# Attention in tiles of 128 queries and one head of each pair, with 64x64 score products

## The chip, the core and the metric

The kernel runs on one core of a Trainium2 chip. The metric is the device time of one execution in microseconds (us), the median of several. The core has a matrix engine (TensorE, PE in the profile; its weight loads stand apart as PEld), three engines for elementwise work (VectorE or DVE, ScalarE or ACT, GpSimd or POOL), and SyncE (SP), which here issues nearly all DMAs. Each engine runs its own list of instructions in order and waits on semaphores for the others. TensorE reads SBUF and writes PSUM; a PSUM tile holds up to 128 partitions by 512 float32.

## The reference, cut to what matters

A windowed attention (2 batches, 8 heads, 768 positions, 64 dimensions a head) is followed by a mixture of experts and a feed-forward layer. Only the attention is touched:

```python
def _attn_ref(q, k, v):
    B, H, S, D = q.shape                      # 2, 8, 768, 64
    block, window = (32, 16)
    nb = S // block                           # 24 blocks of 32 positions
    scale = 1.0 / np.sqrt(D)
    k_sum = k.reshape(B, H, nb, block, D).max(axis=3)
    v_sum = v.reshape(B, H, nb, block, D).mean(axis=3)
    scores_l = scale * np.matmul(q, k.transpose(0, 1, 3, 2))
    mask_l = np.abs(pos[:, None] - pos[None, :]) < window
    scores_s = scale * np.einsum('bhsd,bhnd->bhsn', q, k_sum) + np.log(block)
    scores_l_m = np.where(mask_l, scores_l, -1000000000.0)
    a = softmax(np.concatenate([scores_l_m, scores_s], axis=-1))   # 1e-9 added to the sum
    return np.matmul(a, np.concatenate([v, v_sum], axis=2))
```

The rows of the result go through a router (`logits = x @ w_gate`), experts and a feed-forward layer, whose code is the same before and after.

## The kernel before, in words

Attention works on blocks of 64 queries: such a block needs the 96 keys around it and the 24 block maxima, 120 columns in all. There are 24 blocks j (12 for each batch). `KW` holds for each pair of heads c (two heads of 64 dimensions make 128 partitions) and each block the 120 key columns; `VW` holds the 120 value rows in the same order.

`scores j h` (L272) computes 64 queries of two heads at once: the weights `QB` are a block diagonal of 128x128, with head 0's queries in one corner, head 1's in the other and zeros elsewhere, so that the 128 output rows are 64 queries of head 0 and 64 of head 1. `masked` (L283) adds the mask and takes the row maximum in one VectorE instruction for each pair; `exps` (L294) takes the exponential on ScalarE, one instruction for each pair, which sums the rows too. `norm` (L303) takes the reciprocal of the sums. `p_turn` (L308) transposes the weights on TensorE, `p_out` copies them out of PSUM, and `pv` (L319) multiplies them by the values of both heads (128 columns, of which each row uses 64). `pv_out` (L327) takes the two useful quarters of that product, multiplies them by the reciprocals and writes the output rows `xs`. `x_store` sends a tile of 128 rows to DRAM for the experts, `x_turn`, `x_out`, `logits` (L350) and `logits_out` make the router's logits of it.

Loads: `load` brings 128 partitions of two positions each (runs of 512 bytes), `load_tiles` 128 partitions of one position and 8 heads (runs of 256 bytes). `pairs` and `tiles` transpose them, `k_out` and `q_out` copy them into place, `k_max`, `k_ends` and `k_blocks` make the block maxima and fill the columns that neighbouring blocks share. `v_blocks`, `v_sum`, `v_rows`, `v_rows_out` and `v_means` make the value means and copy them to `VW`, the last of them by 24 DMAs.

The order of all this is written out by hand in the table `ORDER`, one word after the other; within an engine, instructions run in just that order. PSUM has two buffers for each of `ps` (scores), `pt` (turned weights), `po` (products with v) and `ptr` (all other). The router begins (L477) when the logits and the stores to DRAM are complete; the rest of the program follows from there.

Of the kernel before, what the change touches and what calls it, by code (L numbers as in the profile page):

```python
# [52 lines left out]
k_ends 0 1 1 pool; pairs q 0 1 0; pairs q 0 2 1; k_blocks 0 0 0 dve; k_max 0 1 1; load q 0 1 1; v_sum 0 0 0
pool; k_blocks 0 0 1 dve; v_sum 0 1 0 pool; scores 0 0; scores 0 1; q_out 0 1 0 act; load_tiles 1 0; scores 1 0;
scores 1 1; k_blocks 0 1 1 dve; load_tiles 1 1; q_out 0 2 1 act; masked 0 0; exps 0 0; pairs q 0 1 1; masked 0
1; scores 2 0; masked 1 0; exps 0 1; scores 2 1; masked 1 1; scores 3 0; scores 3 1; v_sum 0 0 1 dve; exps 1 0;
load_tiles 1 2; p_turn 0; k_blocks 0 1 0 dve; v_sum 0 1 1 pool; load_v 0 0; tiles 1 0 0; exps 1 1; p_turn 1;
load q 1 0 0; masked 3 0; masked 3 1; masked 2 0; q_out 0 1 1 act; p_out 0 dve; masked 2 1; exps 2 0; load q 1 1
0; scores 4 0; scores 4 1; exps 3 0; pairs q 0 2 0; k_ends 0 2 0 pool; k_out 1 0 0 act; k_ends 0 2 1 dve; exps 2
1; scores 5 0; masked 4 0; exps 3 1; q_out 0 2 0 dve; scores 5 1; p_turn 2; v_rows 0; masked 4 1; scores 6 0;  # L60
k_blocks 0 2 1 pool; tiles 1 0 1; exps 4 0; v_rows_out 0 act; exps 4 1; masked 5 0; exps 5 0; load q 1 0 1; norm
3; k_blocks 0 2 0 pool; masked 5 1; scores 6 1; p_out 1 dve; scores 7 0; p_out 2 act; scores 7 1; p_turn 4;
tiles 1 2 0; masked 6 0; masked 6 1; scores 8 0; scores 8 1; masked 7 0; k_out 1 0 1 act; tiles 1 1 1; exps 5 1;
k_out 1 2 0 act; v_means 0 0; p_out 4 dve; exps 6 0; masked 7 1; k_max 1 0 0; v_blocks 1; scores 9 0; p_turn 3;
k_out 1 1 1 act; exps 6 1; scores 9 1; exps 7 0; tiles 1 1 0; k_max 1 2 0; k_out 1 1 0 act; masked 8 0; masked 8
1; scores 10 0; tiles 1 2 1; p_out 3 act; k_max 1 0 1; k_max 1 1 1; p_turn 5; masked 9 0; masked 9 1; v_sum 1 0
1 pool; k_max 1 1 0; exps 7 1; norm 0; v_means 0 1; pv 0; scores 10 1; k_out 1 2 1 act; load q 1 2 0; norm 2;
exps 9 0; pairs q 1 0 1; pv 1; pv_out 0; k_max 1 2 1; load q 1 1 1; norm 1; k_ends 1 2 2 dve; k_ends 1 0 2 dve;
norm 7; q_out 1 0 1 act; p_turn 6; scores 11 0; norm 4; scores 11 1; p_out 5 act; exps 9 1; pairs q 1 1 0; pairs
q 1 0 0; load_v 0 1; q_out 1 0 0 act; q_out 1 1 0 act; pv_out 1; p_turn 7; v_sum 1 0 0 dve; masked 10 0; pv 2;  # L70
x_turn 0; x_out 0 dve; k_blocks 1 0 2 dve; exps 8 0; masked 10 1; exps 8 1; load q 1 2 1; pv_out 2; exps 10 0;
masked 11 0; norm 5; x_store 0; pv 3; pairs q 1 1 1; pv_out 3; logits 0; scores 12 0; v_means 0 2; q_out 1 1 1
act; norm 6; k_ends 1 1 2 dve; exps 10 1; logits_out 0 act; scores 12 1; p_out 6 act; pv 4; pv 5; pairs q 1 2 0;
masked 11 1; v_sum 1 1 0 pool; masked 12 0; masked 12 1; v_sum 1 1 1 pool; k_blocks 1 2 2 dve; exps 12 0; p_out
7 act; scores 13 0; scores 13 1; pv_out 4; exps 11 0; scores 14 0; masked 13 0; x_store 1; v_rows 1; load_v 1 1;
pv_out 5; p_turn 8; q_out 1 2 0 act; x_store 2; pv 6; v_rows_out 1 dve; exps 12 1; load_v 0 2; masked 13 1;
p_turn 9; pv_out 6; exps 11 1; scores 14 1; norm 10; masked 14 0; p_out 8 act; x_turn 2; pairs q 1 2 1; p_out 9
act; scores 15 0; p_turn 10; x_out 2 act; p_turn 11; masked 14 1; x_turn 1; norm 12; k_blocks 1 1 2 dve; exps 13
0; pv 7; p_out 11 dve; scores 15 1; exps 13 1; pv 8; norm 8; scores 16 0; masked 15 0; scores 16 1; masked 15 1;
x_out 1 act; pv_out 7; q_out 1 2 1 act; exps 14 0; masked 16 0; p_turn 13; p_out 13 dve; scores 17 0; scores 17  # L80
1; masked 16 1; pv_out 8; exps 15 0; logits 1; exps 16 0; norm 9; exps 14 1; p_out 10 act; x_turn 3; masked 17
0; scores 18 0; x_out 3 act; pv 9; load_v 1 0; logits_out 1 dve; masked 17 1; scores 19 0; logits 3; exps 15 1;
p_turn 12; masked 18 0; scores 18 1; exps 16 1; exps 18 0; scores 19 1; exps 17 0; logits 2; norm 11; p_out 12
dve; pv_out 9; p_turn 14; p_turn 15; pv 10; norm 16; masked 18 1; exps 17 1; masked 19 0; p_out 15 act; masked
19 1; logits_out 2 act; v_means 1 0; scores 20 0; norm 15; masked 20 0; exps 18 1; scores 21 0; exps 20 0; later
0; logits_out 3 act; p_out 14 act; x_store 3; pv_out 10; pv 11; scores 20 1; p_turn 16; exps 19 0; masked 21 0;
masked 20 1; norm 13; scores 21 1; p_turn 17; pv_out 11; scores 22 0; pv 12; exps 19 1; x_turn 5; pv 13; masked
21 1; exps 21 0; scores 22 1; x_turn 4; exps 20 1; norm 17; x_out 5 act; v_means 1 2; pv_out 12; norm 14;
x_store 4; logits 5; x_out 4 act; pv_out 13; logits_out 5 dve; exps 21 1; pv 14; masked 22 0; pv 15; p_out 16
act; load_v 1 2; pv_out 14; norm 19; scores 23 0; pv_out 15; v_means 1 1; p_turn 18; logits 4; x_turn 7; p_out  # L90
17 act; logits_out 4 dve; exps 22 0; pv 16; masked 23 0; masked 22 1; p_out 18 dve; p_turn 20; scores 23 1;
x_store 5; x_out 7 act; x_turn 6; exps 22 1; logits 7; pv_out 16; p_turn 19; exps 23 0; p_out 19 act; pv 17;
# [9 lines left out]
def attention(tc, ctx, C, q, k, v, wg, xdram, lg, later, order=ORDER):  # L102
# [979 lines left out]
```

## Time and profile before

| | us |
|---|---|
| median of 3 runs (lowest to highest) | 621.61 (620.71 to 622.36) |
| profiled execution | 620.55 |
| its span | 618.8 |
| TensorE busy, VectorE, ScalarE, GpSimd (of the span) | 595.4, 355.9, 234.4, 143.1 |
| attention: first scores start | 18.83 |
| attention: last logits copied, router starts | 104.73, 105.0 |

The span is what the profile records, from the first instruction to the last; the execution's own time is 1.75 us longer. Attention takes the first 105 us of the span; everything after it is the router, the experts and the feed-forward layer. "Busy" counts the time in which an engine has at least one instruction in work; TensorE's instructions overlap, so that the mean duration of one says less than the distance between the starts of two.

### The profile page before, as it was taken

How to read it: one execution, taken by the hardware profiler on the slowest of the kernel's cores; microseconds unless marked ns; L12 is line 12 of the kernel's file. 1: busy time of each engine (PE TensorE's matmuls, PEld its weight loads, DVE VectorE, ACT ScalarE, POOL GpSimd, SP SyncE). 2: the span in 40 equal slices, each digit the busy share in tenths (PEclk: the TensorE clock that was granted, in tenths of full speed). 3: DMA queues.
4: the chain of work that ended last, by engine and by line, in shares of the span. 5: the costliest groups of instructions: out<-in, count | busy, mean ns of one | idle time of the engine just before them, and what ended most of it. 6: DMA issues, size and time to landing. Idle time of an engine off the chain costs nothing.

```text
span 618.8 us, 10468 instructions
## 1 busy us (share of the span) xinstructions
PE 595.4 (96%) x3883; PEld 530.6 (86%) x3888; DVE 355.9 (58%) x1161; ACT 234.4 (38%) x595; POOL 143.1 (23%) x169
## 2 busy tenths in 40 slices
PE   5898999899999999999999999999999999999996
PEld 3888998458888888889999999999999899999995
DVE  7799887745666655540000699887763544433350
ACT  5998961011122122122222343434343443433342
POOL 7736000011021011010000222223333623333314
PEclk9799999999999999999999999999999999999999
DMA  9998824269686796699600043334400200000002
GB/s 247 213 219 200 173 77 145 95 104 353 139 266 196 181 321 217 118 184 215 198 1 1 11 135 132 134 134 138 136 1 0 103 1 0 2 0 1 2 0 102
DMA packets 79237, 75.68 MB, mean 122 GB/s; under 512 B 30610, under 2 KB 65426, under 8 KB 78802
## 3 DMA queue, kind: packets, MB, share of 16 engines
q1 hardware_dynamic: 76674, 68.70, 41.7%
q0 software_dynamic: 1984, 6.29, 4.2%
q8 instruction: 30, 0.49, 0.4%
q14 instruction: 21, 0.17, 0.1%
q10 hardware_dynamic: 528, 0.02, 0.0%
HBM read 67.52 MB, written 6.30 MB: 119 GB/s over the span
## 4 chain that ended last, share of the span: by engine, by line
PE 86%; DVE 6%; POOL 2%; ACT 2%; issue 1%; DMA 1%; SPq 1%; POOLq 0%; ACTq 0%; DVEq 0%
PE ph L936 21%; PE po L959 19%; PE acc L773 15%; PE acc L780 14%; PE po L324 3%; PE ps L280 3%; PE rt L560 2%; POOL out_dram L985 2%; PE px L709 1%; PE ptr L353 1%; PE pt L312 1%; DMA nat<-in_k_dram 1%; PE rt L681 1%; PE px L755 1%; DVE sb L291 1%
## 5 line engine op out<-in xcount | busy, mean ns | idle before, releaser
L920 POOL TENSOR_TENSOR wl<-wf,wh 128x1024 fp32r<-128x1024 f32 x32 | 77.0, 2405 | 238.1 <-ACT wh L919 230.1
L773 PE MATMUL acc<-xt,w 128*128 128x192 f32 x512 | 95.5, 335 | 0.6 <-ACT xt L756 0.6
L780 PE MATMUL acc<-ht,w 128*128 128x192 f32 x512 | 94.8, 333 | 0.0
L936 PE MATMUL ph<-yh,wh 128*128 128x384 f32 x256 | 87.3, 341 | 0.9 <-PE ph L936 0.9
L936 PE MATMUL ph<-yh,wl 128*128 128x384 f32 x256 | 86.4, 338 | 0.3 <-POOL wl L920 0.3
L936 PE MATMUL ph<-yl,wh 128*128 128x384 f32 x256 | 86.2, 337 | 0.0
L773 PEld LDWEIGHTS acc<-xt,w 128*128 128x128 f32 x512 | 82.1, 190 | 1.7 <-ACT xt L756 0.8
L780 PEld LDWEIGHTS acc<-ht,w 128*128 128x128 f32 x512 | 82.3, 190 | 0.8
L959 PE MATMUL po<-wh,gh 128*128 128x512 f32 x192 | 75.0, 391 | 0.0
L959 PE MATMUL po<-wl,gh 128*128 128x512 f32 x192 | 74.9, 390 | 0.0
L959 PE MATMUL po<-wh,gl 128*128 128x512 f32 x192 | 74.8, 389 | 0.0
L940 DVE TENSOR_SCALAR u<-ph 128x384 f32<-128x384 f32 x64 | 35.3, 552 | 65.5 <-PE ph L936 65.5
L717 POOL DMA_INDIRECT xg<-xdram,idx x16 | 15.6, 974 | 190.1 <-ACT idx L689 94.8
L941 ACT ACTIVATE u<-u,half 128x384 f32<-128x384 f32 x64 | 39.5, 617 | 50.7 <-DVE u L940 50.7
L945 ACT ACTIVATE gh<-u 128x384 fp32r<-128x384 f32 x64 | 33.6, 526 | 59.7 <-DVE u L944 59.7
L767 DVE TENSOR_TENSOR yl<-acc,yh 128x192 fp32r<-128x192 f32 x32 | 11.1, 352 | 70.1 <-ACT yh L785 70.1
L944 DVE TENSOR_TENSOR u<-ph,u 128x384 f32<-128x384 f32 x64 | 35.3, 551 | 26.7 <-ACT u L941 26.7
L936 PEld LDWEIGHTS ph<-yh,wh 128*128 128x128 f32 x256 | 48.1, 188 | 2.5 <-PE ph L936 1.2
L936 PEld LDWEIGHTS ph<-yl,wh 128*128 128x128 f32 x256 | 48.1, 188 | 1.1
L936 PEld LDWEIGHTS ph<-yh,wl 128*128 128x128 f32 x256 | 48.1, 188 | 0.6 <-POOL wl L920 0.6
L919 ACT ACTIVATE wh<-wf 128x1024 fp32r<-128x1024 f32 x32 | 33.9, 1060 | 37.4 <-PE po L959 27.8
L775 ACT ACTIVATE ht<-acc 128x192 f32<-128x192 f32 x64 | 21.1, 329 | 70.9 <-PE acc L773 68.8
(201 smaller groups left out, 908.8 us busy)
## 6 DMA issues: line engine op xcount, KB each, us to landing
w<-in_moe_w_dram SPq DMA_DIRECT2D x31, 1024.0 KB
raw<-in_moe_w_in_dram SPq DMA_DIRECT2D x16, 512.0 KB
raw<-in_moe_w_out_dram SPq DMA_DIRECT2D x16, 512.0 KB
vw<-in_v_dram SPq DMA_DIRECT2D x20, 192.0 KB
nat<-in_k_dram SPq DMA_DIRECT2D x12, 256.0 KB
nat<-in_q_dram SPq DMA_DIRECT2D x12, 256.0 KB
vn<-in_v_dram SPq DMA_DIRECT2D x4, 768.0 KB
xdram<-xs SPq DMA_DIRECT2D x12, 256.0 KB
```

The lines of the kernel that those rows point to most:

```text
L280: nc.tensor.matmul(live["s", j][:, c, :120], QB[slot(b, g)][:, c, ii, :], KW[b][:, g, c, ii, :], start=True, stop=True)
L773: nc.tensor.matmul(p, w[:, c, f % 4 * 128:f % 4 * 128 + 128], xt[:, c], start=(c == 0), stop=(c == 3))
L775: nc.scalar.activation(ht[:, f], p, AF.Relu)
L780: nc.tensor.matmul(p, w[:, f, c % 2 * 128:c % 2 * 128 + 128], ht[:, f], start=(f == 0), stop=(f == 7))
L919: nc.scalar.activation(h, a, AF.Copy)
L920: nc.gpsimd.tensor_tensor(l, a, h.bitcast(F32), op=OP.subtract)
L936: nc.tensor.matmul(p, w[:, c * 128:(c + 1) * 128], y[half][:, c, s], start=(k == 0), stop=(k == 11))
L940: nc.vector.tensor_scalar(u, p, 1.0, -1.0, op0=OP.min, op1=OP.max)
L941: nc.scalar.activation(u, u, AF.Square, bias=self.half, scale=0.5)
L944: nc.vector.tensor_tensor(u, p, u, op=OP.max)
L945: nc.scalar.activation(gh[:, s], u, AF.Copy)
L959: nc.tensor.matmul(po[t], x[:, s], w[:, 512:], start=(f == 0 and i == 0), stop=(f == self.FB - 1 and i == 2))
```

## The change

Attention works on tiles of 128 queries t (12 of them), and on one head of each pair, a = 0 or 1, at a time: a PSUM tile holds 128 queries by 4 pairs by 120 columns. The scores are 16 products of 64 queries by 64 dimensions by 120 columns for each tile, each in one quarter of TensorE's array (row half a, column half w). The mask is put into PSUM ahead of them by a product of a bfloat16 identity with the mask row, 480 columns wide. `masked` gives way to `top` (the row maxima of all four pairs, one VectorE instruction) and `less` (subtract them, one instruction); `exps` is one ScalarE instruction of 480 columns where `less` stands in the table (18 of 24 times), or four of 120 with the maximum as bias where it doesn't (6 times). The row sums come from `pv`: each value block has a 65th column of ones (32 for the block means, which are now sums over 32 rows; so log 32 is no longer added). `pv` is 16 products of 64 queries by 65 columns for each tile, and `logits` is split in the same way into halves of 64 rows. `sums` adds 1e-9. `QB` with its zeros is gone; `QT` holds q turned. `v_means` becomes three GpSimd copies for each batch instead of 24 DMAs in all. All loads of the first batch's q and k are `load_tiles`. The table is written anew.

```diff
@@ table (its first and last words)
-begin; load k 0 0 0; load k 0 1 0; load k 0 2 0; pairs k 0 0 0; load q 0 0 0; load k 0 1 1; load k 0 0 1; k_out
+begin; load_tiles k 0 2; load_tiles k 0 1; later 0; tiles k 0 2 1; tiles k 0 2 0; k_out 0 2 1 act; load_tiles q
...
-    QB = [st.tile([128, HP, 4, 128], F32, name=f"qb{n}") for n in range(4)]
-    VW = [st.tile([120, 4, H, D], F32, name=f"vw{n}") for n in range(4)]
+    QT = [st.tile([128, HP, 256], F32, name=f"qt{n}") for n in range(B * G)]
+    VW = [st.tile([120, 4, H, D + 1], F32, name=f"vw{n}") for n in range(4)]
...
-    def v_means(b, g):
-        for ii in range(4):
-            nc.sync.dma_start(VW[slot(b, g)][96:120, ii], VM[b].rearrange("p (h d) -> p h d", d=D))
+    def v_means(b, g, eng):
+        e = nc.vector if eng == "dve" else nc.gpsimd
+        e.tensor_copy(VW[slot(b, g)][96:120, :, :, :D],
+                      VM[b][96:120, None].to_broadcast([NB, 4, DM]).rearrange("p i (h d) -> p i h d", d=D))
...
+    def scores(t):
+        b, i = divmod(t, NT // B)
+        m = bias[0 if i == 0 else 2 if i == NT // B - 1 else 1]
+        s = live["s", t] = [pp.tile([128, HP, 120], F32, name="ps") for _ in range(2)]
+        for a in range(2):
+            nc.tensor.matmul(s[a], identb, m[:, None].to_broadcast([128, HP, 120]), start=True, stop=False,
+                             skip_group_check=True)
+        for c in range(HP):
+            for w, a in ((0, 0), (1, 1), (0, 1), (1, 0)):
+                r = slice(64 * a, 64 * a + 64)
+                n = 128 * (i % 2) + 64 * w
+                nc.tensor.matmul(s[a][64 * w:64 * w + 64, c], QT[b * G + i // 2][r, c, n:n + 64],
+                                 KW[b][r, i // 2, c, n // 64], start=False, stop=True, skip_group_check=True)
+
+    def top(t, a):
+        m = live["m", t, a] = wk.tile([128, HP], F32, name="mx", bufs=4)
+        nc.vector.tensor_reduce(m, live["s", t][a], axis=AX.X, op=OP.max, negate=True)
+
+    def less(t, a):
+        m = live["m", t, a]
+        sb = live["d", t, a] = wk.tile([128, HP, 120], F32, name="sb")
+        nc.vector.tensor_tensor(sb, live["s", t][a], m[:, :, None].to_broadcast([128, HP, 120]), op=OP.add)
+
+    def exps(t, a):
+        pr = live["e", t, a] = wk.tile([128, HP, 120], F32, name="pr", bufs=5)
+        if ("d", t, a) in live:
+            nc.scalar.activation(pr, live.pop(("d", t, a)), AF.Exp)
+            return
+        for c in range(HP):
+            nc.scalar.activation(pr[:, c], live["s", t][a][:, c], AF.Exp, bias=live["m", t, a][:, c:c + 1])
...
+    def pv(t, a):
+        b, i = divmod(t, NT // B)
+        pt = live.pop(("ts", t, a))
+        po = live["p", t, a] = pp.tile([128, HP, 128], F32, name="po")[:, :, :D + 1]
         for c in range(HP):
-            nc.tensor.matmul(po[:, c], pt[:, c], VW[slot(b, i // 4)][:, i % 4, 2 * c:2 * c + 2], start=True, stop=True)
+            for w in range(2):
+                n = 2 * (i % 2) + w
+                nc.tensor.matmul(po[64 * w:64 * w + 64, c], pt[:, c, 64 * w:64 * w + 64],
+                                 VW[slot(b, i // 2)][:, n, 2 * c + a], start=True, stop=True)
+
+    def sums(t, a, eng):
+        rs = live["rs", t, a] = wk.tile([128, HP], F32, name="rs", bufs=4)
+        if eng == "act":
+            nc.scalar.activation(rs, live["p", t, a][:, :, D], AF.Identity, bias=eps)
+        else:
+            nc.vector.tensor_scalar(rs, live["p", t, a][:, :, D], 1e-9, None, op0=OP.add)
...
+        nc.vector.tensor_tensor(o, po[:, :, :D], rs[:, :, None].to_broadcast([128, HP, D]), op=OP.mult)
...
     def logits(t):
         p = live["l", t] = ptr()
         for c in range(4):
-            nc.tensor.matmul(p[:, 0, :64], live["xt", t][:, c], wg[:, c], start=(c == 0), stop=(c == 3))
+            for w in range(2):
+                r = slice(64 * w, 64 * w + 64)
+                nc.tensor.matmul(p[r, 0, :64], live["xt", t][:, c, r], wg[:, c], start=(c == 0), stop=(c == 3))
```

TensorE in the second half of attention, before (`ps` scores, `pt` turned weights, `po` products with v, `ptr<-ident,xs` the output rows turned, `ptr<-wg,xt` logits; the x4 of `po` and `pt` are the four pairs of heads of one block, the x2 of `ps` is half a block's):

```order
L312 MATMUL pt<-ident,pr 120x128 x4
L280 MATMUL ps<-kw_89,qb_91 128x120 x2
L324 MATMUL po<-vw_97,ptS 128x128 x4
L344 MATMUL ptr<-ident,xs 128x128 x4
L324 MATMUL po<-vw_97,ptS 128x128 x4
L280 MATMUL ps<-kw_89,qb_91 128x120 x2
L344 MATMUL ptr<-ident,xs 128x128 x4
L353 MATMUL ptr<-wg,xt 128x64 x4
```

And in the changed kernel, one tile of 128 queries in the same half, from the second of its two masks (`ps<-bias,identb`) on:

```order
L283 LDWEIGHTS identb
L283 MATMUL ps<-bias_109,identb 128x480
L289 MATMUL ps<-kw_89,qt_94 64x120 x16
L313 MATMUL pt<-ident,pr 120x128 x4
L355 MATMUL ptr<-ident,xs 128x128 x4
L313 MATMUL pt<-ident,pr 120x128 x4
L327 MATMUL po<-vw_96,ptS 64x65 x8
L366 MATMUL ptr<-wg,xt 64x64 x8
L327 MATMUL po<-vw_96,ptS 64x65 x8
```

Products over the whole array, with transposes among them, now alternate with products in quarters (L289) and in halves (L327, L366), and a tile's scores stand in one piece instead of in halves of a block.

VectorE in the second half of attention, before (L291 is `masked`, its second row the read-out of the maximum; L334 is `pv_out`):

```order
L291 ISA sb,nm<-ps,bias_107 128x120
L291 ISA nm 128x1
L305 TENSOR_SCALAR rs<-rs 128x4
L306 RECIPROCAL rs<-rs 128x4
L129 COPY ptS<-pt 120x512
L334 TENSOR_TENSOR xs<-po,rs 64x4x64 x2
```

And in the changed kernel (L294 is `top`, L299 `less`, L335 `sums`):

```order
L294 TENSOR_REDUCE mx<-ps 128x4 x2
L127 COPY ptS<-pt 120x512
L299 TENSOR_TENSOR sb<-ps,mx 128x480 x2
L335 TENSOR_SCALAR rs<-po 128x4 x2
L338 RECIPROCAL rs<-rs 128x4 x2
```

Both maxima of a tile now stand together behind its scores, with the copy of an earlier tile's weights between them and the two subtractions.

SyncE's first loads, before (`nat` is q or k as it lies in DRAM, `vn` are blocks of v for the means):

```order
L142 DMA nat<-in_k_dram 128x4x128 x3
L142 DMA nat<-in_q_dram 128x4x128
L142 DMA nat<-in_k_dram 128x4x128 x2
L142 DMA nat<-in_q_dram 128x4x128 x2
L142 DMA nat<-in_k_dram 128x4x128
```

And in the changed kernel:

```order
L150 DMA nat<-in_k_dram 128x8x64 x4
L150 DMA nat<-in_q_dram 128x8x64 x2
L150 DMA nat<-in_k_dram 128x8x64 x2
L173 DMA vn_257<-in_v_dram 96x2048
L173 DMA vn_258<-in_v_dram 96x2048
```

Each load of q or k is 256 KB; 128x8x64 moves runs of 64 float32, 128x4x128 runs of 128. All eight now stand ahead of the first scores.

## Rows read from the trace of the kernel before

**Rows 1.** busy time by stage: stretch, length, engines, granted clock, DMA share, GB/s

```profile
0.00:18.80 18.80, 10.87 (x50) 7.16 (x51) 13.78 (x33) 11.89 (x28) 13.28 (x30) 0.83 0.99 243
18.80:50.00 31.20, 27.95 (x231) 26.38 (x229) 28.15 (x131) 29.61 (x117) 17.24 (x36) 0.94 1.02 208
50.00:102.30 52.30, 51.67 (x465) 50.61 (x464) 45.57 (x221) 35.85 (x144) 7.56 (x32) 1.00 0.57 133
102.30:105.00 2.70, 2.40 (x20) 2.26 (x20) 0.10 (x1) 0.95 (x3) 0.00 (x0) 1.00 0.67 208
```

**Rows 2.** chain of waits: start us, duration us, what, instructions

```profile
5.75 5.68 DMA nat<-in_k_dram
18.83 3.41 PE ps L280 x16
...
67.77 0.44 PE ptr L344 x4
68.21 0.44 PE ps L280 x4
68.65 0.90 PE po L324 x8
...
70.19 0.85 PE ptr L353 x8
71.03 0.44 PE pt L312 x4
...
102.59 2.44 DMA xdram<-xs
105.02 0.24 DVE m L477
```

**Rows 3.** TensorE's groups of matmuls, 18.8 to 102.3: xcount | busy, mean ns

```profile
L280 PE MATMUL ps<-kw,qb 128*128 128x120 f32 x192 | 28.3, 289 | 0.6 <-DVE nm L291 0.5
L213 PE MATMUL ptr<-ident,nat 128*128 128x128 f32 x33 | 5.4, 290 | 0.4 <-ACT pr L300 0.4
L220 PE MATMUL ptr<-ident,nat 128*128 128x128 f32 x24 | 3.6, 273 | 0.0
L195 PE MATMUL ptr<-vsum,ident 96*24 96x64 f32 x32 | 2.1, 220 | 0.0
```

**Rows 4.** timeline of TensorE's matmuls around a change of tile shape: start, duration

```profile
55.97 0.50 PE L280 MATMUL ps<-kw,qb 128*128 128x120 f32 x3
56.40 1.07 PE L195 MATMUL ptr<-vsum,ident 96*24 96x64 f32 x16
57.40 0.54 PE L312 MATMUL pt<-ident,pr 128*120 128x128 f32 x3
```

**Rows 5.** the same timeline at an earlier place, cut within a group

```profile
30.71 0.39 PE L195 MATMUL ptr<-vsum,ident 96*24 96x64 f32 x4
```

**Rows 6.** timeline of TensorE's weight loads beside Rows 4

```profile
56.39 0.91 PEld L195 LDWEIGHTS ptr<-vsum,ident 96*24 96x24 f32 x16
```

**Rows 7.** groups of VectorE and ScalarE, 18.8 to 102.3: xcount | busy, mean ns

```profile
L291 DVE CUSTOM_DVE_ANT_0 sb<-ps,bias 128x120 f32<-128x120 f32 x96 | 21.9, 277 | 5.7 <-PE ps L280 4.0 <-ACT pr L300 1.2
L334 DVE TENSOR_TENSOR xs<-po,rs 64x256 f32<-64x256 f32 x48 | 20.1, 420 | 1.4 <-PE po L324 0.8
L247 DVE TENSOR_REDUCE ks<-kw 128x16 f32<-128x512 f32 x6 | 3.9, 678 | 0.0
...
L300 ACT ACTIVATE pr<-sb,nm 128x120 f32<-128x120 f32 x96 | 36.5, 384 | 3.7 <-DVE nm L291 3.6
```

**Rows 8.** two stretches of loading, 512-byte runs, then 256-byte; columns as before

```profile
6.00:12.00 6.00, 2.29 (x20) 1.84 (x19) 3.12 (x7) 4.77 (x12) 5.05 (x12) 1.00 1.21 293
20.00:25.00 5.00, 5.00 (x36) 5.00 (x36) 3.63 (x18) 4.86 (x21) 4.61 (x8) 0.74 1.35 219
```

**Rows 9.** chain of waits in the router: bfloat16 matmuls of 512 columns

```profile
122.76 2.26 PE px L709 x10
```

**Rows 10.** timeline of ScalarE at the end of attention

```profile
104.73 0.18 ACT L127 ACTIVATE lg<-ptr 128x8 f32<-128x8 f32 x1 [0.78 <-PE ptr L353]
```

More of the change, by code (lines that the diff above doesn't have):

```diff
@@ L53 @@
[L53 to L92, printed above, removed]
@@ new lines @@
+less 1 1; load_v 0 1; p_out 0 0 act; top 1 0; exps 1 1; less 1 0; v_rows_out 0 act; p_turn 1 1; scores 2; exps 1
+0; v_means 0 0 pool; p_out 1 1 dve; tiles q 0 2 1; top 2 0; tiles q 0 2 0; v_means 0 2 pool; load_tiles k 1 1;
+q_out 0 2 1 act; top 2 1; pv 0 0; q_out 0 2 0 act; pv 0 1; less 2 1; sums 0 0 act; exps 2 0; p_turn 1 0; norm 0
+0; pv_out 0 0; v_means 0 1 pool; p_out 1 0 dve; pv 1 1; load q 1 0 0; sums 0 1 act; scores 3; exps 2 1; norm 0
+1; pv_out 0 1; load q 1 2 0; sums 1 1 dve; norm 1 1; pv_out 1 1; pv 1 0; load_tiles k 1 0; top 3 1; x_turn 0;
@@ new lines @@
+sums 1 0 act; top 3 0; exps 3 1; tiles k 1 1 1; p_turn 2 1; less 3 0; p_turn 2 0; p_out 2 1 dve; p_out 2 0 act;
+scores 4; x_out 0 dve; x_store 0; exps 3 0; norm 1 0; load q 1 0 1; k_out 1 1 1 act; pv_out 1 0; pv 2 1; top 4
+0; load_v 0 2; logits 0; sums 2 1 dve; k_max 1 1 1; x_turn 1; logits_out 0 act; p_turn 3 0; less 4 0; tiles k 1
+1 0; p_out 3 0 act; x_out 1 dve; pv 2 0; k_out 1 1 0 act; top 4 1; logits 1; exps 4 0; sums 2 0 dve; tiles k 1 0
+1; norm 2 0; logits_out 1 act; p_turn 4 0; pv_out 2 0; k_out 1 0 1 act; load_tiles k 1 2; tiles k 1 0 0; less 4
@@ new lines @@
+1; p_out 4 0 act; p_turn 3 1; norm 2 1; scores 5; k_out 1 0 0 act; pv_out 2 1; k_max 1 1 0; p_out 3 1 act;
+k_ends 1 1 2 pool; k_max 1 0 0; exps 4 1; x_turn 2; x_store 2; top 5 1; pv 3 0; k_ends 1 0 2 pool; x_out 2 act;
+top 5 0; v_blocks 1; pv 3 1; exps 5 1; sums 3 0 dve; logits 2; norm 3 0; pv_out 3 0; tiles k 1 2 0; k_max 1 0 1;
+p_turn 4 1; logits_out 2 act; sums 3 1 act; tiles k 1 2 1; k_out 1 2 0 act; norm 3 1; p_turn 5 1; pv_out 3 1;
+p_out 4 1 act; k_max 1 2 0; x_turn 3; k_out 1 2 1 act; pv 4 1; p_out 5 1 dve; x_out 3 act; k_ends 1 2 2 pool;
@@ new lines @@
+x_store 5; x_turn 4; top 6 1; logits 5; load q 1 2 1; x_out 4 dve; exps 6 1; logits_out 5 dve; load q 1 1 1;
+logits 4; top 6 0; pairs q 1 1 0; logits_out 4 dve; load_v 1 1; less 6 0; p_turn 6 1; v_rows 1; q_out 1 1 0 dve;
+p_out 6 1 act; exps 6 0; scores 7; v_rows_out 1 act; v_means 1 0 pool; p_turn 6 0; top 7 1; pairs q 1 1 1; p_out
+6 0 act; top 7 0; pairs q 1 2 1; load_v 1 2; q_out 1 1 1 act; less 7 0; v_means 1 1 pool; pv 6 1; less 7 1; pv 6
+0; sums 6 1 dve; q_out 1 2 1 act; scores 8; norm 6 1; pv_out 6 1; v_means 1 2 pool; sums 6 0 dve; norm 6 0;
@@ L326, in pv_out, with p_out @@
[L326 to L335 removed]
+    def p_out(t, a, eng):
+        sb = live["ts", t, a] = wk.tile([120, HP, 128], F32, name="ptS", bufs=5)
+        evac(eng, sb, live.pop(("t", t, a)))
```

175 lines of the change are left out of this document (79 added, 96 removed).

## The prediction, made before the changed kernel was run

> **What bounds the kernel now.** I read the busy times by stage first, then the chain of waits through attention, then the groups of each engine there, and last the timeline of single matmuls where the shape of the product changes. Only attention is touched, so everything hangs on when the router starts: at 105.0 us now. From 50 to 102.3 TensorE is busy 51.67 of 52.30 us [rows 1]; the chain there runs from one TensorE group to the next. VectorE has 45.57 and ScalarE 35.85 of the same stretch. From 18.8 to 50 all three are near full (27.95, 28.15 and 29.61 of 31.2). So the loads of VectorE and ScalarE count early, TensorE's later, and what TensorE is left with late is what it could not start early.
>
> TensorE's price is the distance between starts. A float32 product shows as two matmul records (192 for 96 products of scores), a transpose as one [rows 3]. Four records of scores take 0.44 us, four transposes 0.44, eight of the products with v 0.90, eight of the logits 0.85 [rows 2]: 0.106 to 0.11 a record, whatever the width between 64 and 128 columns. Only the products with few weights go faster: four records of 64 columns with 24 weights last 0.39 us with the last lasting 0.22 by itself [rows 3, 5], so (0.39 - 0.22) / 3 = 0.057 a record.
>
> TensorE's work from the first scores at 18.83 [rows 2] to the last logits: scores 192 x 0.11 = 21.1, products with v 192 x 0.1125 = 21.6, logits 96 x 0.106 = 10.2, turned weights and rows 144 x 0.11 = 15.8, q and k turned (33 + 24) x 0.11 = 6.3 [rows 3], value means 2.0 (twice 16 in 1.00 [rows 4]), together 77.0. The first 16 score records took 3.41 instead of 1.76 because the granted clock stood at its lower level, 1.2 GHz (0.83 and 0.94 on average in the first two stages, 1.00 after [rows 1]): 1.7 more, 78.7. The stretch lasts until the last logits are copied at 104.73 [rows 10], 85.9 us, so TensorE waits 7.2 us in it.
>
> **The change on TensorE.** Gone are 96 score products over the whole array; 192 in quarters come. Neither a quarter nor two halves working beside each other has a row here. Bounds for a score quarter: both records 0.11 with nothing beside, 0.22 a product; all four quarters beside each other, 0.055. I take the middle, 0.11: the two records of a product use the same quarter and follow one another, but the next product uses another row half or column half, or both, and its first record can run beside the second of this one. 192 x 0.11 = 21.1, as before. Products with v and logits: 192 + 96 in halves of 64 weights and 64 or 65 columns. By the narrow-weight row 0.057 a record; nothing beside 0.114 a product, the neighbour's half beside 0.057. I take 0.057 by the same reasoning: 288 x 0.057 = 16.4 instead of 31.8. New are 24 masks of 480 bfloat16 columns; ten of 512 take 2.26 us [rows 9], so 24 x 0.226 x 480/512 = 5.1. Turned weights, rows, q and k: 96 + 48 + 64 transposes (the other 32 fall before the first scores), 208 x 0.11 = 22.9. Value means 2.0. And new is the change of shape: between the last score record and the first with 24 weights lie 0.43 us for three records instead of 0.33, and at the end of those 57.40 - (56.40 + 15 x 0.057) = 0.15 instead of 0.057 [rows 4]. So each change costs 0.09 to 0.10. Whole, quarter and half products alternate 64 times in the changed order: 5.8 us. That agrees with the Trainium skill, TensorEngine Tiling (Array Packing), section Tiling Modes, by which a change of mode drains the engine; the page gives no price, so the row's stands in the sum. Together 21.1 + 16.4 + 5.1 + 22.9 + 2.0 + 5.8 = 73.3, and 1.7 for the low clock at the start again: 75.0, 3.7 less than before.
>
> The halves are the weakest term. The Trainium skill, TensorE: Matmul & The Clock Gate, section The mechanism, says that a weight load overlaps a running matmul only where the row group differs. Two halves of the product with v use the same rows. Here the trace differs where it can be seen: the 16 weight loads with 24 columns run all through the 16 matmuls with the same rows, 0.91 us in 1.07 [rows 4, 6]. That doesn't show two halves beside each other, so the rule stands below as a rival.
>
> **VectorE and ScalarE.** Gone on VectorE: 96 masked maxima, 21.9 us, and half of the 20.1 us of output products, which become 24 of 128 partitions in place of 48 of 64 with the same 256 columns [rows 7]. New: 24 maxima and 18 subtractions of 480 columns. A maximum over 512 took 678 ns [rows 7], for 480 I take 0.64; a subtraction lies between an output product of 256 (0.42) and the same 678; I take 0.64 too: 42 x 0.64 = 26.9. Net 26.9 - 21.9 - 10.0 = -5.0 of 73.8 [rows 1]. On ScalarE 96 exponentials with 36.5 us busy [rows 7] become 18 of 480 columns and 24 of 120. The price of a wide one is at most 4 x 0.384 and I take 0.64 as for VectorE: 11.5 + 9.2 = 20.7, 16 less, more with the read-out of the sums gone. This is work that binds only before 50 us. There it lets TensorE do more early, and this is why I don't let its waits grow.
>
> What could make them grow: both score buffers now belong to one tile, and the next tile's masks wait for its two maxima and two subtractions, 4 x 0.64 = 2.6 us. Behind the waiting mask nothing else on TensorE can start. The order puts about 3 us of turned weights, rows, logits and products with v ahead of it (12 x 0.11 + 8 x 0.057 + 16 x 0.057 = 2.7, with three changes of shape 3.0), so the wait is mostly covered: scores with masks 16 x 0.11 + 0.43 = 2.2, then 3.0 of other work against VectorE's 2.6 plus a copy of 0.7. I leave TensorE's waits at 7.2, between 4 (ScalarE and VectorE lighter) and 14 (half a microsecond more at each tile).
>
> **Loads and the start.** Two megabytes now stand ahead of the first scores in runs of 256 bytes. Such loads went at 219 GB/s, runs of 512 bytes at 293 [rows 8]. Now the ninth load of 256 KB ends at 11.43 [rows 2]: 2.36 MB / 293 = 8.1 us of it transfer. Eight at 219 take 9.6, so the last k lands near 12.9. Behind it come four transposes at the low clock (0.9), two maxima (0.68 each [rows 7]), a copy of as many columns that I take to cost the same, and nine small copies on GpSimd (my estimate 0.23 each, a quarter above ScalarE's 0.18 for eight columns [rows 10]): 5.0, with handovers 5.6, so 18.5 for the first scores, within 1.5 either way; now 18.83. The value means no longer take 24 DMAs but six GpSimd copies, where GpSimd is idle for over 40 of the last 52 us and 14 of the 31 before [rows 1]; if a first copy is late, the first product with v is, which the waits contain.
>
> The end keeps its form: the last output rows go to DRAM (2.44 us) and only then does the router start [rows 2].
>
> **The sum.** 18.5 + 75.0 + 7.2 = 100.7 for the last logits, 101 for the router, 4.0 earlier than 105.0. The profiled execution took 620.55 with a span of 618.8: 616.5. Its own time is 1.06 below the median of 621.61, on which this is **617.5**.
>
> **Rivals.**
> 1. Quarters and halves run freely beside each other. Scores 192 x 0.055 = 10.6, TensorE 64.5. Then VectorE bounds: first maximum near 22, its 68.8 us of work, then the store: 22 + 69 + 3 = 94, eleven earlier: 610.5. For: nothing in the operands of two quarters is shared. Against: the two records of a product share theirs.
> 2. Halves of the product with v don't overlap (by the rule above the second half's weights wait): 288 x 0.114 = 32.8 instead of 16.4. TensorE 91.4; it then waits less, 4: 18.5 + 91.4 + 4 = 114, nine later: 630.5. For: the row of 0.106 for logits with 64 columns, where the weights and not the columns set the pace [rows 2]. Against: those were 128 weights; with 24 the pace is the columns'.
> 3. Nothing overlaps: 42.2 + 32.8 for the products, TensorE 112.5, router near 134: 650.
> 4. The slower end by another mechanism: the shared pair of score buffers. If each of eleven tiles waits 0.6 us more for its maxima and subtractions than I cover, waits are 14 and the router starts at 107.8: 624. It decides from 4 us of added waits in all, where the gain is gone.
>
> **Chances.** Forecast (613 to 620) 0.45; first rival 0.15; second 0.14; third 0.06; fourth, with times from 620 to 626, 0.20. A measurement here tells apart about 0.3%, 1.9 us. Faster by more: nearly all of the forecast and the first rival, 0.58. Within: the rest of the forecast and the near part of the fourth, 0.15. Slower: 0.27. Range 609 to 631: it leaves out the third rival and the best of the first. The forecast's own range is 613 to 620.
>
> **What would show it.** In the changed profile: 32 score records of a tile in about 1.8 us (1.0 for the first rival, 3.5 for the third); 16 records of a product with v in about 0.46 us, 0.9 for the second; gaps near 0.09 at each change of shape; first scores near 18.5; TensorE idle near 7 us to the end of attention, in pieces ahead of the masks if the fourth holds. The forecast is wrong if the router starts after 103 or before 97.

## The result, and the profile after

The changed kernel takes 611.71 us (median of four runs, 610.55 to 611.89), the kernel before 621.79 in the same series: ratio 0.9836, 95% interval 0.9818 to 0.9854. It is 10.1 us faster. The forecast was 617.5, 4 faster: the direction held, the size did not. Of the profiled execution (610.55 us) the span is 608.4 us, 10.4 less than before, and the router starts at 94.42 instead of 105.02 [rows 2], 10.6 earlier. What follows the router's start takes 514.0 us now and 513.8 before, so all of the gain lies in attention: 1.6 of the 10.6 is the earlier start of the scores (17.24, before 18.83), 9.0 the shorter stretch from there to the last logits' copy (76.9, before 85.9).

Busy time by stage in the changed kernel (stretch, its length; then PE, PEld, DVE, ACT, POOL with instruction counts; granted clock; DMA share; GB/s), to be held against [rows 1]:

```profile
18.80:50.00 31.20, 28.31 (x454) 22.43 (x447) 25.87 (x49) 17.26 (x43) 12.56 (x20) 0.85 1.00 210
50.00:94.40 44.40, 40.88 (x747) 32.89 (x745) 34.70 (x86) 30.35 (x74) 15.71 (x28) 1.00 0.62 153
```

TensorE is still the fullest engine: 69.2 us of the 75.6 after 18.8, VectorE has 60.6, ScalarE 47.6. The clock is lower in the first of these two stretches than before (0.85, before 0.94), which comes back below.

TensorE's part of the chain of waits around two tiles and at the end (start, duration, what, number of records), against [rows 2]:

```profile
35.24 0.51 PE ps L283 x2
35.76 0.98 PE ps L289 x32
36.74 0.62 PE po L327 x16
...
40.63 0.62 PE po L327 x16
41.25 0.47 PE ptr L366 x16
...
92.01 0.67 PE ptr L355 x4
92.76 0.61 ACT xt L125
93.41 0.71 PE ptr L366 x16
94.14 0.19 ACT lg L125
94.42 0.26 DVE m L492
```

In this view a group lasts from the end of the one ahead of it to its own end, so that a change of shape ahead of it counts with it. A tile's 32 score records (16 products, two records each) take 0.98 us, the change of shape between masks and scores included. Sixteen records of products with v take 0.62 where they follow the scores, with a change of shape; sixteen of the logits right behind them, in the same shape, take 0.47. At the end it is the logits of the last tile that the router waits for: their copy ends at 94.33. The last store to DRAM, which ended attention before, lands at 94.20, just ahead of it.

The groups of each engine, 17.2 to 94.3 us (count | busy, mean ns of one | idle before), against [rows 3, 7]:

```profile
L327 PE MATMUL po<-vw,ptS 120*64 120x65 f32 x384 | 15.5, 226 | 0.3 <-DVE ptS L127 0.2
L294 DVE TENSOR_REDUCE mx<-ps 128x4 f32<-128x480 f32 x24 | 15.2, 652 | 4.6 <-PE ps L289 4.6
L289 PE MATMUL ps<-kw,qt 64*64 64x120 f32 x384 | 14.3, 293 | 2.9 <-DVE kw L273 2.9
L299 DVE TENSOR_TENSOR sb<-ps,mx 128x480 f32<-128x480 f32 x18 | 11.6, 654 | 0.8
L304 ACT ACTIVATE pr<-sb 128x480 f32<-128x480 f32 x18 | 10.7, 603 | 0.1
L346 DVE TENSOR_TENSOR xs<-po,rs 128x256 f32<-128x256 f32 x24 | 10.1, 424 | 1.2
L283 PE MATMUL ps<-bias,identb 128*128 128x480 bf16 x22 | 6.9, 387 | 0.7 <-DVE sb L299 0.7
L307 ACT ACTIVATE pr<-ps,mx 128x120 f32<-128x120 f32 x24 | 6.7, 368 | 0.5 <-DVE mx L294 0.5
```

The prices of VectorE and ScalarE that I had to guess were right within 0.04 us: 0.652 and 0.654 for the wide maximum and subtraction (0.64 taken), 0.603 for the wide exponential (0.64). The masks waited for VectorE 0.7 us in all (the row of L283), so the fourth rival, a wait for the shared score buffers at every tile, did not happen.

### The profile page after: what moved, and what is told of

Same layout as the page of the kernel before. It is cut to its first block, busy times and chain, and to the rows that moved or that the text cites. A ratio compares the mean times of both kernels' runs of the same rounds, so it can differ in the third digit from the quotient of the medians.

```text
span 608.4 us, 11078 instructions
## 1 busy us (share of the span) xinstructions
PE 583.5 (96%) x4392; PEld 506.8 (83%) x4392; DVE 338.6 (56%) x956; ACT 208.0 (34%) x427; POOL 146.8 (24%) x188
## 4 chain that ended last, share of the span: by engine, by line
PE 87%; DVE 4%; POOL 2%; ACT 2%; DMA 2%; SPq 1%; issue 1%; POOLq 0%; DVEq 0%; ACTq 0%
PE ph L951 22%; PE po L974 19%; PE acc L788 15%; PE acc L795 14%; PE rt L575 2%; PE pt L313 2%; PE po L327 2%; PE px L724 2%; DMA vn<-in_v_dram 2%; PE ps L289 2%; POOL out_dram L1000 2%; SPq L150 1%; PE ptr L366 1%; PE ptr L355 1%; PE rt L696 1%
## 5 line engine op out<-in xcount | busy, mean ns | idle before, releaser
L935 POOL TENSOR_TENSOR wl<-wf,wh 128x1024 fp32r<-128x1024 f32 x32 | 76.9, 2404 | 238.1 <-ACT wh L934 238.1
L790 ACT ACTIVATE ht<-acc 128x192 f32<-128x192 f32 x64 | 21.1, 330 | 70.8 <-PE acc L788 70.8
```

The costliest lines, as they stand in the source:

```text
L790: nc.scalar.activation(ht[:, f], p, AF.Relu)
L935: nc.gpsimd.tensor_tensor(l, a, h.bitcast(F32), op=OP.subtract)
```

## The experiments

Of twelve variants five changed the order of the products inside a tile or a group and so tell what TensorE does beside what; two changed its masks; one moved an instruction on VectorE and one kept TensorE busy at the start; two joined these to the cheaper masks; and one took a single part of the change into the kernel before. The five orders were timed once each; the kernel before took 620.65 on the same chip (620.92 for the order in twos). One correction holds for the runs quarter by quarter, in the same rows or columns, half by half and with other masks: their expectations count 24 tiles, or 48 groups, but there are 12 tiles of 16 products and 24 groups of one tile and one head of each pair. The work per tile or group is as they say, the sum half of it.

**Quarter by quarter.**

```diff
-        for c in range(HP):
-            for w, a in ((0, 0), (1, 1), (0, 1), (1, 0)):
+        for w, a in ((0, 0), (1, 1), (0, 1), (1, 0)):
+            for c in range(HP):
```

> The changed kernel with the 16 products of a tile's scores ordered quarter by quarter: four products of one quarter, then four of the next. Theory A (every quarter runs its own records one after another at 0.1025 us for 120 columns, and all four quarters run beside each other): 32 records take 32 x 0.1025 = 3.3 us a tile in place of 0.82, 24 x 2.46 = 59 us more TensorE work, nearly all of it seen at the end: 650 to 671. Theory F (the forecast's: a product's first record runs beside the second of the product before, where the quarter differs): it should have read 1.76 a tile before and 3.3 now. Theory C (nothing runs beside anything, a record with 64 weights and 64 rows is simply cheap, 0.026): the order means nothing, 0.82 a tile, 611.7. Theory R (a weight load overlaps only where the rows differ): 3.3 as A.

**Neighbours in the same rows** (first) **or the same columns** (second).

```diff
+        for a in range(2):
+            for c, w in [(c, w) for c in range(HP) for w in range(2)]:
...
+        for w in range(2):
+            for c, a in [(c, a) for c in range(HP) for a in range(2)]:
```

> The changed kernel with a tile's score products ordered so that neighbours share the row half and alternate between the two column halves (8 products of row half 0, then 8 of row half 1). Theory A: two quarters at a time, 32 records in 16 x 0.1025 = 1.64 us a tile, 24 x 0.82 = 20 us more TensorE work, the end 10 to 20 later: 622 to 632. Theory C: 0.82, 611.7. Theory R (same rows: no overlap of the weight load): one quarter at a time, 3.3 us a tile, as the serial order, 650 to 671.

> The changed kernel with a tile's score products ordered so that neighbours share the column half and alternate between the two row halves. Theory A: 1.64 us a tile, 622 to 632, as with the same rows. Theory C: 0.82, 611.7. Theory R: the rows differ from product to product, so 1.64 or less, 611.7 to 632. If two row halves of the same columns could not run together it would be 3.3 us, 650 to 671.

**In twos of one quarter.**

```diff
+        for c2 in range(HP // 2):
+            for c, w, a in [(2 * c2 + d, w, a) for w, a in ((0, 0), (1, 1), (0, 1), (1, 0)) for d in range(2)]:
```

> The changed kernel with a tile's score products ordered in twos of one quarter (A A B B C C D D, so four records of a quarter stand in a row). Theory A' (records of a quarter queue up to four deep behind its running one while those of the next quarter start, as the quarter-by-quarter run showed: it started the second quarter after the fifth record of the first): 32 records take 0.9 to 1.0 us a tile, 12 tiles, at most 2 us more TensorE work: 611 to 613.5. Theory F (the forecast's, strict order: a record waits for the one of the same quarter before it and holds up all behind it): 1.6 or more a tile, 10 us more TensorE work, 619 to 622.

One tile of scores in each, from TensorE's timeline (start, duration, records), with the row that follows; the distance of the two starts is the tile's price. First the changed kernel, then quarter by quarter, same rows, same columns, in twos:

```profile
35.69 1.05 PE L289 MATMUL ps<-kw,qt 64*64 64x120 f32 x32
36.67 0.69 PE L327 MATMUL po<-vw,ptS 120*64 120x65 f32 x16
```

```profile
39.44 2.43 PE L289 MATMUL ps<-kw,qt 64*64 64x120 f32 x32
41.80 0.40 PE L327 MATMUL po<-vw,ptS 120*64 120x65 f32 x6
```

```profile
37.28 1.51 PE L289 MATMUL ps<-kw,qt 64*64 64x120 f32 x32
38.72 0.45 PE L327 MATMUL po<-vw,ptS 120*64 120x65 f32 x8
```

```profile
36.44 1.51 PE L289 MATMUL ps<-kw,qt 64*64 64x120 f32 x32
37.88 0.51 PE L327 MATMUL po<-vw,ptS 120*64 120x65 f32 x10
```

```profile
34.28 1.11 PE L289 MATMUL ps<-kw,qt 64*64 64x120 f32 x32
35.33 0.69 PE L327 MATMUL po<-vw,ptS 120*64 120x65 f32 x16
```

So 0.98, 2.36, 1.44, 1.44 and 1.05 us, with the change of shape behind the tile in each. If nothing ran beside anything, the order would mean nothing, so Theory C falls. If an overlap needed different rows, the same-rows order would cost what quarter by quarter does; it costs what the same columns do, so Theory R falls for these quarters. Strict order (Theory F) would have made the twos 1.6 or more; they cost 0.07 more than the changed kernel. What is left is that every quarter takes its own records one after another, at 0.1025 us for 120 columns, and that all four go side by side. The quarter-by-quarter tile was cheaper than the 3.3 that this gives, and the starts of its single records say why (us, the tile of the rows above; records of the first quarter, then of the second, told apart by their even distances):

```
39.435 39.589 39.691 39.794 39.896         39.999 40.101 40.204
39.902 40.055 40.158 40.260 40.363 ...
```

The second quarter starts 6 ns behind the fifth record of the first, while three records of the first are still to come. A few records of a busy quarter can wait without holding up those behind them. The record that reports the end of the third quarter bears this out: it starts at 41.137, behind the first three of the fourth (40.835, 40.989, 41.091). So a new quarter begins every 0.467 us, the last takes 0.87 for its eight records, and a change of shape follows: 3 x 0.467 + 0.87 + 0.09 = 2.36. At the one border of the orders in pairs the same happens, which is why they take 1.44 and not the 1.64 expected.

Times: quarter by quarter 627.15 us, same rows 615.88, same columns 615.38, in twos 609.62. In the first of these orders the change is a loss against the kernel before. The last is no gain: its first tile's maximum was 1.2 us earlier because a load had landed earlier, and from the third tile on it was slower (below).

**Products with v, half by half.**

```diff
-        for c in range(HP):
-            for w in range(2):
+        for w in range(2):
+            for c in range(HP):
```

> The changed kernel with a group's eight products with v ordered half by half: four of column half 0, then four of column half 1. Theory A (the two column halves run beside each other, a record of 65 columns 0.058 in its half): 16 records take 0.94 us in place of 0.47, 48 x 0.47 = 22 us more TensorE work, the end 12 to 22 later: 624 to 634. Theory C or R (they run one after another as it is, 0.029 a record): no change, 611.7.

```profile
35.16 0.94 PE L327 MATMUL po<-vw,ptS 120*64 120x65 f32 x16
36.04 0.58 PE L283 MATMUL ps<-bias,identb 128*128 128x480 bf16 x2
```

A group takes 0.87 us (35.165 to 36.038 by its single records) in place of 0.62 (36.667 to 37.283 in the changed kernel), and the time is 617.10. The halves run beside each other too: my price for them, 0.057 a product, held, and the second rival falls.

**Mask products twice, and masks in quarters.**

```diff
-        for a in range(2):
+        for a in (0, 1, 0, 1):
             nc.tensor.matmul(s[a], identb, m[:, None]...
```

```diff
+        for w in range(2):
+            for a in range(2):
+                r = slice(64 * a, 64 * a + 64)
+                nc.tensor.matmul(s[a][64 * w:64 * w + 64], identb[r, r],
+                                 m[w][r, None].to_broadcast([64, HP, 120]), start=True, stop=False, ...
```

(Cut: `m` now holds a mask row for each column half w, and the two edge masks are written for all 128 rows.)

> The changed kernel with each tile's two mask products issued twice (the second pair overwrites the first, the values are the same): 0.41 us more TensorE work a tile, 24 x 0.41 = 9.8 us, with no new wait for data. If TensorE bounds all of attention the end moves by 9.8: 621.5. If it bounds only where it has no idle time (30 to 54 and 72 to 90 us, some 15 of the 24 tiles), by 5 to 7: 617 to 619. If another engine or the loads bound it, by less than 2: 612 to 613.7.

> The changed kernel with each mask product over the whole array cut into quarter products (64 rows of the identity and of the mask), four a tile, each in the quarter that its scores use. By the theory that quarters run beside each other, the masks of a tile take 0.20 in place of 0.41, and the change of shape between masks and scores (0.09) goes: 0.30 a tile, 7.2 us less TensorE work; 4 to 6 of it at the end: 606 to 608. If bfloat16 quarters do not overlap: four of 0.20 are 0.80 a tile, less the change of shape 0.09: 0.3 more a tile, 615 to 618.

The two kernels in that order:

```profile
34.92 0.98 PE L283 MATMUL ps<-bias,identb 128*128 128x480 bf16 x4
35.84 1.05 PE L289 MATMUL ps<-kw,qt 64*64 64x120 f32 x32
```

```profile
33.42 0.40 PE L285 MATMUL ps<-bias,identb 64*64 64x480 bf16 x4
33.65 0.99 PE L292 MATMUL ps<-kw,qt 64*64 64x120 f32 x32
```

From the first mask to the first score it is 0.51 us in the changed kernel (35.18 to 35.69), 0.92 with the masks doubled, 0.23 in quarters. The doubled masks took 615.67 us (615.28 to 615.99; ratio to before 0.9910, 0.9895 to 0.9926), the quarters 607.26 (607.01 to 607.58; 0.9777, 0.9763 to 0.9790). The second beats both kernels of the case: bfloat16 quarters run side by side as the float32 ones do (four start within 10 ns), and no change of shape stands between masks and scores. In its profiled run the router starts 4.0 us earlier than in the changed kernel's; 1.7 of that lies ahead of the third tile, where a load of value rows had landed 2.2 earlier (below), so that not all of it is shown to be the masks'.

**The sum of value rows later, alone and with the masks in quarters.**

```diff
-scores 0; v_sum 0 0 1 pool; v_sum 0 1 1 dve; load_v 0 0; top 0 0; ...
+scores 0; v_sum 0 0 1 pool; load_v 0 0; top 0 0; ...
-less 0 1; exps 0 0; v_sum 0 1 0 dve;
+less 0 1; exps 0 0; v_sum 0 1 1 dve; v_sum 0 1 0 dve;
```

> The changed kernel with one VectorE sum of value rows (1.89 us, waiting for its load until 19.98) moved from before the first row maxima to behind the first tile's subtractions. If that load holds up the start: the first maximum starts at 19.1 instead of 21.8, and the end comes 1.5 to 2.7 us earlier: 609 to 610.2. If the later loads (q of the second 256 queries, k of the second batch) set the pace of that stretch, nothing: 611.7.

> Both edits, the masks in quarters and the sum of value rows moved. If their gains are in different stretches they add up: 604 to 607. If TensorE's shorter tiles only turn into longer waits for VectorE or for loads: as the better of the two alone, 606 to 611.

VectorE at the first tile, in the changed kernel and with the sum moved (the bracket says what ended the wait):

```profile
19.98 1.89 DVE L182 TENSOR_REDUCE vsum<-vn 96x32 f32<-96x1024 f32 x1 [2.13 <-DMA vn<-in_v_dram]
21.78 0.65 DVE L294 TENSOR_REDUCE mx<-ps 128x4 f32<-128x480 f32 x1
```

```profile
18.31 0.66 DVE L294 TENSOR_REDUCE mx<-ps 128x4 f32<-128x480 f32 x1 [1.35 <-PE ps L289]
19.00 0.66 DVE L299 TENSOR_TENSOR sb<-ps,mx 128x480 f32<-128x480 f32 x1
```

The first maximum comes 3.5 us earlier (0.9 of it because the scores start at 16.36 in this run), the third tile's scores 2.9 (27.84 instead of 30.72), and the router starts at 91.58. The median is 609.73, 2.0 below the changed kernel, but the runs spread from 607.97 to 613.68 and the interval of the ratio (0.9810 to 0.9858) covers the changed kernel's, so the timing alone does not show the gain; the trace does for its own run. With both edits it was 607.23 (605.55 to 610.78), no better than the masks in quarters alone. In the profiled run of it TensorE waited 1.88 us for GpSimd's sum of the second batch's value rows, and the granted clock behind that gap was at its lower level for a while (0.57 on average from 63 to 67, 1.00 ahead of it):

```profile
60.00:63.00 3.00, 1.16 (x14) 0.85 (x9) 2.39 (x7) 1.09 (x2) 2.67 (x5) 1.00 1.01 271
63.00:67.00 4.00, 3.96 (x54) 3.43 (x55) 0.07 (x1) 0.59 (x1) 1.47 (x1) 0.57 0.98 171
```

```profile
63.04 1.80 PE L194 MATMUL ptr<-vsum,ident 96*24 96x64 f32 x16 [1.88 <-POOL vsum L188]
64.77 0.61 PE L285 MATMUL ps<-bias,identb 64*64 64x480 bf16 x4
65.17 1.69 PE L292 MATMUL ps<-kw,qt 64*64 64x120 f32 x32
```

This tile's scores took 1.62 (65.17 to 66.79), with the masks in quarters alone 0.92 (62.27 to 63.19). That this is what spreads the runs was not tried.

**TensorE kept busy at the start, alone and with the masks in quarters.**

```diff
+    def heat(n):
+        for _ in range(n):
+            nc.tensor.matmul(pp.tile([128, 512], F32, name="po"), x[:, :128], x, start=True, stop=True)
...
+heat 3; tiles k 0 0 1; heat 3; tiles k 0 0 0; ... heat 14; scores 0; heat 8; ... heat 3; scores 1;
```

> The changed kernel with 31 bfloat16 products of zeros, 512 columns each, into a free buffer of TensorE's results, put into TensorE's idle time between 10 and 25 us. If the granted clock then stays at 1.0 to 28 us (it is 0.50 from 15 to 27 now): scores, turned weights and masks of the first two tiles cost half, 2 to 3 us less TensorE work before 28.5, and 1 to 2.5 at the end: 609 to 610.7. If that is only given back as a longer wait for loads at 54 to 63 us: 611.2 to 612. If the clock falls all the same or the products delay the first scores: 612 to 614.

> The masks in quarters and the 31 products of zeros together. If both gains are TensorE's and add up: 604.5 to 606.5. If the wait for loads in the middle takes the second: 607, as the masks in quarters alone.

Two stretches of the changed kernel, then of the heated one:

```profile
12.00:18.80 6.80, 3.16 (x41) 2.40 (x41) 4.77 (x22) 0.60 (x1) 4.16 (x17) 0.69 1.03 231
18.80:28.00 9.20, 6.58 (x56) 4.45 (x49) 7.26 (x8) 2.40 (x5) 4.85 (x10) 0.50 0.98 190
```

```profile
12.00:18.80 6.80, 6.76 (x61) 3.37 (x60) 4.81 (x22) 0.52 (x1) 4.89 (x18) 1.00 1.04 235
18.80:28.00 9.20, 6.79 (x77) 4.43 (x75) 8.39 (x10) 4.43 (x8) 4.18 (x9) 1.00 1.05 208
```

In the changed kernel, TensorE busy 3.16 of the first 6.80 us, the clock fell to 1.2 GHz (0.50) before 15 us and stayed there until past 28; in the heated one, busy 6.76 of 6.80, it kept 2.4. The third tile's scores came at 28.57 instead of 30.72, 0.6 of it because the load ahead of the first sum landed earlier (19.39 instead of 19.98). The time was 608.65 (606.74 to 610.50; ratio 0.9795, 0.9773 to 0.9818): 3.1 lower, with intervals that touch. On top of the masks in quarters it gave 606.73 (606.15 to 608.80; 0.9773, 0.9754 to 0.9791), nothing that can be told from 607.26.

**The logits in halves in the kernel before.**

```diff
-            nc.tensor.matmul(p[:, 0, :64], live["xt", t][:, c], wg[:, c], ...
+            for w in range(2):
+                r = slice(64 * w, 64 * w + 64)
+                nc.tensor.matmul(p[r, 0, :64], live["xt", t][:, c, r], wg[:, c], ...
```

> The kernel before with one part of the change alone: the logits in column halves, 64 weights each. By the price of halves in the changed kernel (16 records in 0.47 to 0.5 us in place of 8 in 0.85) 12 x 0.35 = 4.2 us less TensorE work, less two changes of shape at 0.09 each in most of the twelve places (2.2): 2.0 net. If TensorE binds where the logits stand (from 35 us on): 619.2 to 620.5, 1 to 2 less than before. If halves gain nothing outside the changed order: 621.2 or up to 2 more.

```profile
65.88 0.69 PE L355 MATMUL ptr<-wg,xt 128*64 128x64 f32 x16
66.50 0.66 PE L344 MATMUL ptr<-ident,xs 128*128 128x128 f32 x4
```

0.62 us a tile with the change of shape behind it, in place of 0.85 [rows 2]; the time 619.66, ratio 0.9978 (0.9965 to 0.9991), 1.3 less. One part alone works, a little: by the prices above the products spare 0.38 a tile (0.85 less 0.47), and the changes of shape on both sides take back about half.

**What a microsecond of TensorE is worth.** The third tile's first score and the router's start bound a stretch that the loads of the start leave alone. It holds ten tiles of scores and all 24 groups of products with v.

| kernel | third tile to router, us | against 63.7 | TensorE's work changed by |
|---|---|---|---|
| changed | 30.7 to 94.4: 63.7 | | |
| quarter by quarter | 33.1 to 109.9: 76.8 | +13.1 | 10 x 1.38 = 13.8 |
| same rows | 31.9 to 99.7: 67.8 | +4.1 | 10 x 0.46 = 4.6 |
| same columns | 31.0 to 98.8: 67.8 | +4.1 | 10 x 0.46 = 4.6 |
| v half by half | 31.1 to 99.7: 68.6 | +4.9 | 24 x 0.26 = 6.2 |
| masks twice | 30.5 to 98.3: 67.8 | +4.1 | 10 x 0.41 = 4.1 |
| in twos | 29.3 to 93.5: 64.2 | +0.5 | 10 x 0.07 = 0.7 |
| masks in quarters | 29.0 to 90.4: 61.4 | -2.3 | -10 x (0.28 + 0.06) = -3.4 |
| sum moved | 27.8 to 91.6: 63.8 | +0.1 | 0 |
| heated | 28.6 to 92.3: 63.7 | 0.0 | 0 |
| masks in quarters, heated | 28.7 to 90.1: 61.4 | -2.3 | -3.4 |
| masks in quarters, sum moved | 29.0 to 94.0: 65.0 | +1.3 | -3.4, and the wait of 1.88 at 63.0 |

Apart from the last row, between 0.7 and 1.0 of what TensorE is given or spared there arrives at the end. (In quarters a tile's scores are 0.06 cheaper too: 0.92 from 33.65 to 34.57.) The sum and the heating act ahead of it alone.

## Why the prediction was right in direction and wrong in size

**What bounds.** That everything hangs on the router's start, and that TensorE sets it, held (the table above). The first rival named VectorE as the next bound; it was busy 60.6 of 75.6 us, so that rival's price was right and its bound was not. How much of the gain the lighter work of VectorE and ScalarE gave was not tried by itself.

**The step that failed** is the price of a score quarter: "I take the middle, 0.11: the two records of a product use the same quarter and follow one another, but the next product uses another row half or column half, or both, and its first record can run beside the second of this one." Measured: four records every 0.1025 us, that is 0.051 a product, at the lower of my two bounds. The first half of the sentence is true, a quarter does its records in turn. The second is not: the next products need not wait for the second record to start, since records of a busy quarter queue and those of the others pass them. 192 x (0.11 - 0.051) = 11.3 us of TensorE were counted too many. The Trainium skill, TensorEngine Tiling (Array Packing), section Tiling Modes, says that different tiles of the array can load weights and multiply in parallel; I cited that section for the change of mode and did not weigh this sentence, which speaks for the first rival. The runs agree with it: 0.98 a tile in the kernel's order, 1.44 two by two. The rule that the forecast did weigh (the Trainium skill, TensorE: Matmul & The Clock Gate, section The mechanism), that a weight load overlaps only where the row group differs, would make same rows dearer than same columns; both took 1.44, so it does not hold here.

With that one price mended the forecast's sum would be 617.5 - 11.3 = 606.2, and the measurement is 5.5 above. Where that went, from the starts of single matmul records between the first score (17.24) and the last logits (a group's last record is counted at its kind's pace, up to 0.1 behind it as change of shape, the rest as waiting):

| TensorE, us | forecast | measured |
|---|---|---|
| scores, low clock at the start included | 21.1 + 1.7 | 12.1 |
| products with v, logits | 16.4 | 12.1 + 5.9 |
| masks (two of 24 ran before the first score) | 5.1 | 4.5 |
| turned weights, rows, q, k | 22.9 | 25.5 |
| value means | 2.0 | 1.8 |
| changes of shape | 5.8 (64) | 5.9 (62) |
| waits | 7.2 | 8.8 |
| sum | 82.2 | 76.6 |

The rest is spread. The table is 5.7 over the mended sum; 1.3 of that came back because the first scores started earlier, and about 1 was added behind the last logits and outside the span. The 5.7 are 2.6 in the turned tiles and 1.6 in the halves, part of it the low clock, which lasted until past 28 us and not only through the first scores, and 1.6 in waits; the small terms nearly cancel. Of these 8.8 us of waiting 4.1 fall before 26.9; the profile puts 1.9 of them down to loads of q and 0.7 to VectorE. Behind VectorE's part, which the chain of waits follows there, lies a place that I had missed: the order puts a sum of value rows, which waits for a load until 19.98, ahead of the first maximum. The run with the sum moved bounds its price, at most 2.9 us at the third tile. The first scores came at 17.2, 1.3 earlier than I said, but the maximum behind them was held until 21.8, so this start won nothing by itself.

**What held besides.** The change of shape at 0.09 to 0.10, the halves at 0.057 to 0.06, the wide VectorE and ScalarE instructions. The end did not keep the form that I said it would: the copy of the last logits and not the store comes last, by 0.1 us.

**The rivals.** The first (quarters free, 610.5) came nearest to 611.7, with a chance of 0.15 where the forecast had 0.45; but its time was counted from VectorE's work, so that it came so near is in part luck. The second and third fell with the halves and the tiles, the fourth with 0.7 us of waits at the masks. My own test in the prediction, wrong if the router starts before 97, has come out: 94.42.

The heating and the moved sum each bring the third tile 2 to 3 us earlier alone and add nothing to the masks in quarters. The profiled runs show why for themselves. VectorE's first sum of value rows in the changed kernel, with the masks in quarters, and with these and the heating:

```profile
19.98 1.89 DVE L182 TENSOR_REDUCE vsum<-vn 96x32 f32<-96x1024 f32 x1 [2.13 <-DMA vn<-in_v_dram]
17.77 1.94 DVE L182 TENSOR_REDUCE vsum<-vn 96x32 f32<-96x1024 f32 x1 [0.41 <-DMA vn<-in_v_dram]
19.66 1.91 DVE L182 TENSOR_REDUCE vsum<-vn 96x32 f32<-96x1024 f32 x1 [1.56 <-DMA vn<-in_v_dram]
```

From the end of that sum to the third tile's scores it is 9.3 us with the masks in quarters (to 29.02) and 7.1 with the heating (to 28.69): 2.2 less, and the load, landing 1.9 later, took nearly all of it back. With the sum moved as well, the first scores started at 18.00 instead of 16.77 and the third tile came at 28.98. Why that load moves by two microseconds between kernels that issue it alike stays open, and so does whether it does so in every run.

## What to carry to other kernels

Where products need only a quarter or half of TensorE's array, write them so that neighbours in the order use different quarters, all four in turn: it was worth 1.4 us a tile here against quarter by quarter, and where their rows or columns meet did not matter. Put small helpers such as a mask into the same tile shape, for each change of shape cost 0.09 to 0.10 us here. Before trusting a sum over one engine, look through the queue of each engine that feeds its first product for an instruction that waits for a load: one such line held the third tile back by up to 2.9 us here, where the score quarters spared TensorE some ten.

## What the runs showed of the hardware

- A float32 product of 120 columns is two records of 0.1025 us in its 64x64 quarter; the four quarters take one each in the same 0.1025. Starts of four such records lay within 20 ns.
- Matmul records of one quarter were passed by those of the next: with the products ordered quarter by quarter, the second quarter began while three records of the first had not started.
- bfloat16 products of 480 columns in four quarters: 0.23 us from the first to the score behind them, about as much as one over the whole array (0.20 to 0.21 to the next).
- In one run TensorE waited 1.88 us and then worked at the lower clock for a while (0.57 on average from 63 to 67): the score tile at 65.17 took 1.62 us in place of 0.92.
- A load of value rows that all these kernels issue alike landed between 17.8 and 20.2 us in ten profiled runs.
